# A two-layer FNet and sliding-window attention kernel: the Newton steps of attention's row norms move to GpSimd, the far scores' region is preset once, rows are asked for four visits ahead, and even visits do their norm step at their end

## The chip, the cores and the metric

The kernel runs on one core of a Trainium2 chip. The core has a matrix engine (TensorE, PE in the profile; the loading of its weights is listed as PEld), a vector engine (VectorE, DVE), a scalar engine (ScalarE, ACT), GpSimd (POOL), and SyncE (SP), which issues nearly all DMA transfers here. The metric is the device time of one execution in microseconds (us); lower is better. Matrices collect their sums in PSUM, which the matrix engine writes and which DVE and ACT read; everything else on the chip lies in SBUF.

## The reference

Four blocks over a stream `x` of 2048 rows by 640 columns, each with a layer norm in front and a residual sum behind: spectral mixing, attention, spectral mixing, attention.

```python
def _A_ref(x, dft_seq_re, dft_seq_im, dft_hid_re, dft_hid_im):      # spectral
    a = jnp.einsum("bsd,ed->bse", x, dft_hid_re)
    b = jnp.einsum("bsd,ed->bse", x, dft_hid_im)
    return jnp.einsum("ts,bse->bte", dft_seq_re, a) - jnp.einsum("ts,bse->bte", dft_seq_im, b)

def _B_ref(x, wqkv, wo):                                            # attention, 32 heads of 20, window 256
    ...
    scores = jnp.einsum("bhqd,bhkd->bhqk", q, k) * (Dh ** -0.5)
    mask = (idx[:, None] - idx[None, :] >= 0) & (idx[:, None] - idx[None, :] < W)
    scores = jnp.where(mask[None, None], scores, -1e9)
    p = _softmax(scores, axis=-1)
    o = jnp.einsum("bhqk,bhkd->bhqd", p, v)
    return (...) @ wo

x = A_x
x = x + _A_ref(_layernorm(x), ...)
x = x + _B_ref(_layernorm(x), B_wqkv, B_wo)
x = x + _A_ref(_layernorm(x), ...)
x = x + _B_ref(_layernorm(x), B_wqkv, B_wo)
```

Two things of it matter below. A layer norm needs 1/sqrt(variance + eps) of every row. And a query at row t sees the 256 keys that end at t: for a tile of 128 queries these lie in three tiles of 128 keys, its own, the one before it, and a triangle of the one before that (the *far* tile). The first two query tiles have no far tile.

## The kernel before, in words

**Stages.** Spectral mixing (`spectral`) takes 0 to 555 us of the span and again some 1060 to 1565 us; attention (`attention`) takes the rest. The change is in attention alone, which runs twice; both runs are called the first and the second attention.

**Visits.** Attention is one loop, `for G in range(...)`, and each pass is called a visit here, numbered from 0 to 127 (`g` = 2G counts pairs of heads). A visit treats one query tile and four heads. Sixteen visits make a block `b` of 256 rows, with two query tiles that alternate: even visits take the first, odd visits the second. In visit G the matrix engine computes

- the scores of visit G by query (`scores`): into `sq` for the two near key tiles, and for the far tile into the first 256 columns of `sk`, the region that the code calls `farq`,
- the scores of visit G-8 by key (`by_key`), into the other columns of `sk`, which ACT turns into probabilities (L1212, `ptq`) and GpSimd cuts to the window (`affine_select`, L1216 and L1218),
- on odd visits the product of probabilities and values (`values`, `pf<-ptq,v`) of visits G-11 and G-10, and
- one *fill*: a unit of 15 dense matmuls that has nothing to do with the visit. A fill is a sixth of the query or key projection of a block to come (called QK: `pf<-early,big`, 128x256), a quarter of its value projection (V: `pf<-big,early`, 128x320), or half an output projection of a finished tile (OUT: `pf<-bo,ot`).

DVE takes the largest score of each query (`largest`): for each of two halves, `copy_predicated` (L1156) lays the far scores over the masked triangle of the diagonal tile, and a `tensor_reduce` (L1158) takes the maximum. There is one `sq` buffer per half, so the matrix engine can write the scores of the next visit only when DVE has reduced those of this one. In visits 0 to 15, whose queries have no far tile, the copy reads `neg`, a constant tile in SBUF.

**Row norms.** Blocks 0 and 1 of the rows are made ready before attention begins. For each of the blocks 2 to 7, `rows_norm` makes the normalised rows from which QK and V fills are computed: two tiles of 128 rows are loaded (`x<-x2d`), `norm_steps` takes mean and variance (L139, L142), then 1/sqrt by a guess from the bits (L148, L149) and three Newton steps of two `tensor_scalar` on one column each (L151, L152), then the rows are scaled (L166), split in a high and a low half (`rx`, ACT L177 and GpSimd L178) and turned by a transposing DMA (`early<-rx`).

**What sets the order.** The code is written in order of visits, and a scheduling layer then places each engine's instructions. `norm_steps` is a generator: each `yield` ends a step, and `slow_step` runs one step. `STEPS` says how many steps a visit runs: one in even visits, two in odd ones, and one more in each of visits 0 to 6. `slow_step` holds its instructions behind the visit's last reduction (`topped[0]`) and behind ACT's last listed instruction. A block's norm starts four units of `g` (two visits) after its rows were asked for; in visit 0 the rows of block 2 are asked for at once. Which fill a visit gets is worked out when the program is written: a unit is ready once its rows have a due visit behind them (`done`, set `TURN_LAG` = 6 units after the transposing DMA), and the ready one with the earliest `due` is taken. A visit without a ready unit gets no fill.

The output projection's sum with the residual stream, L935 (`x<-pf,beta,x`), frees the PSUM buffer of an OUT fill; there are two such `pf` buffers, shared by all fills, the values and the small transposes.

Of the kernel before, what the change touches and what calls it, by code (L numbers as in the profile page):

```python
# [46 lines left out]
STEPS = ((1, 2), (1, 2))  # L47
# [3 lines left out]
FREE_STEPS = 4  # L51
PIECES = 2
# [20 lines left out]
def body(ctx: ExitStack, tc: tile.TileContext, x_in, cmat, whid, wqkv, wo, out):  # L73
# [15 lines left out]
    neg = pers.tile([P, P], F32, name="neg")  # L89
# [4 lines left out]
    def constants():  # L94
        make_identity(nc, idf[:])
        nc.vector.tensor_copy(idh, idf)
        nc.gpsimd.memset(mask, 1)
        nc.gpsimd.memset(neg, NEG)
        nc.gpsimd.memset(shift, SHIFT)
        for k in range(2):  # L100
            nc.gpsimd.memset(ones[:, k], M_UP if k else 0.0)
            nc.sync.dma_start(ones_d[k].rearrange("a (b c) -> (a b) c", c=2 * NP * QB // P), ones[:, k])
        nc.gpsimd.affine_select(out=mask, in_=mask, pattern=[[1, P]], base=0, channel_multiplier=-1,
                                compare_op=OP.is_gt, fill=0.0)
# [27 lines left out]
    def norm_steps(xs, ys, act=False):  # L132
# [13 lines left out]
        for k in range(n):  # L146
# [677 lines left out]
    def attention(layer, proj, dst, final):  # L824
        with ExitStack() as st:
# [12 lines left out]
            tps = [t[:, 2 * P:].rearrange("p (a e c) -> p e a c", a=3, e=2) for t in kst]  # L838
            in_turn[0] = True
# [82 lines left out]
            def out_tile(i):  # L922
                ot = OT[i]
                x3 = x2 = X2.pop(i)
                for n in range(2):
# [9 lines left out]
                    nc.vector.scalar_tensor_tensor(x3[:, cs], pf[:, :320], beta, x2[:, cs], op0=OP.mult, op1=OP.add)  # L935
# [66 lines left out]
            def rows_norm(b, x2s):  # L1002

                ys = []
                yield from norm_steps(x2s, ys)
# [143 lines left out]
            def largest(G, pi):  # L1149
# [4 lines left out]
                far = farq[pi] if i >= 2 else neg[:, None, :].to_broadcast([P, 2, P])  # L1154
                with in_line("dve"):
                    marks["dve"] = nc.vector.copy_predicated(near[pi][:, :, 0], mask[:, None, :].to_broadcast([P, 2, P]), far).ins  # L1156
# [140 lines left out]
            def slow_step():  # L1297
                with tc.issue_after(topped[0]), in_line("act"):
# [19 lines left out]
            for G in range(NS // 2 + 1):  # L1318
# [38 lines left out]
                if wanted and x2s and g >= x2s[0] + 4 * (g > 0):  # L1357
                    slow.append(rows_norm(wanted.pop(0), x2s.pop()))
                    x2s.clear()
# [19 lines left out]
                for _ in range(STEPS[layer][G % 2] + (g < ROWS_STEP)):  # L1379
                    slow_step()  # L1380
# [18 lines left out]
                if ran and turned_back:  # L1399
                    with in_line("dve"):  # L1400
                        back(turned_back.pop())
            while unit[0] is not None or fill or slow or idle or later:
# [39 lines left out]
```

## Time and profile before

| | |
|---|---|
| median of 3 runs (lowest, highest) | 2056.11 us (2054.0, 2058.06) |
| the profiled execution's own time | 2055.16 us |
| its span, first to last instruction | 2053.4 us |
| first attention, scores from | 555.5 us on |
| second attention, scores from | 1565.4 us on |
| mean granted TensorE clock | 0.996 |

The time and the span of the profiled execution differ by 1.8 us that lie outside the instructions. In the views below a row of the timeline gives start, duration, engine, line, operation and tiles, with the idle time of the engine ahead of it and what ended that in square brackets. A row of the view of windows gives, for a stretch of time, its length and then each engine's busy time with its number of instructions, the granted clock of the matrix engine, and the share of the DMA engines. A row of the groups gives busy time in us and the mean of one instruction in ns behind the first bar.

### The profile page before, as it was taken

What the parts mean: (1) busy time and instruction counts of PE and PEld (TensorE: products, weight loads), DVE (VectorE), ACT (ScalarE), POOL (GpSimd) and SP (SyncE); (2) the same over time, 40 slices, a digit from 0 to 9 for tenths busy, and PEclk for the clock granted to TensorE, in tenths of its full rate; (3) what the DMA queues carried; (4) which work ended last, traced back from release to release, by engine and by line L of the source; (5) the groups of instructions that cost most, each with busy time, mean ns of one, the idle gap of its engine ahead of it and who ended that gap; (6) DMA issues with size and microseconds to landing.
All of it is one profiled execution on the core that took longest, in us unless ns stands there. A gap on an engine that the chain in (4) does not pass through costs nothing.

```text
span 2053.4 us, 55784 instructions
## 1 busy us (share of the span) xinstructions
PE 1987.5 (97%) x21881; PEld 1449.1 (71%) x21881; DVE 1563.3 (76%) x3261; ACT 1115.0 (54%) x1973; POOL 1469.2 (72%) x2162
## 2 busy tenths in 40 slices
PE   6999999999999999999999999999999999999998
PEld 4777777776767777777667777777677677777765
DVE  8888778768688888777638779787777788887682
ACT  5544555533347677666654444444332567766674
POOL 5777788877557788776557778777783677777653
PEclk9999999999999999999999999999999999999999
DMA  7556566566544444434535565454844455443222
GB/s 274 178 197 202 175 209 228 179 240 216 154 108 111 121 122 121 103 85 111 158 132 179 171 165 186 147 174 139 300 148 131 99 118 123 124 120 98 76 68 72
DMA packets 280508, 311.10 MB, mean 152 GB/s; under 512 B 107572, under 2 KB 214836, under 8 KB 271156
## 3 DMA queue, kind: packets, MB, share of 16 engines
q1 hardware_dynamic: 279668, 306.88, 50.2%
q8 instruction: 171, 2.80, 0.6%
q14 instruction: 93, 0.76, 0.1%
q10 hardware_dynamic: 576, 0.66, 0.1%
HBM read 201.72 MB, written 83.46 MB: 139 GB/s over the span
## 4 chain that ended last, share of the span: by engine, by line
PE 68%; DVE 16%; issue 5%; POOL 4%; ACT 4%; DMA 3%; SPq 0%; DVEq 0%; ACTq 0%; POOLq 0%
PE pf L126 32%; PE y L126 10%; PE x L126 10%; PE z L126 7%; PE sk L126 5%; DVE cc L536 4%; PE sq L126 3%; DVE sq L1156 2%; DVE m L1158 2%; DMA res<-accd 2%; ACT ptq L1212 2%; DVE lnst L139 1%; DVE res L559 1%; DVE lnt L151 1%; POOL cs L526 1%
## 5 line engine op out<-in xcount | busy, mean ns | idle before, releaser
L126 PEld LDWEIGHTS <-cc 128*128 128x128 f16 x5376 | 524.4, 98 | 214.4 <-issue 14.7
L1212 ACT ACTIVATE ptq<-sk,shift,alpha 128x768 f32<-128x768 f32 (+2 forms) x512 | 471.9, 944 | 125.9 <-PE sk L126 74.7
L126 PEld LDWEIGHTS <-big 128*128 128x128 f16 x4320 | 414.3, 98 | 129.3 <-issue 24.2
L1158 DVE TENSOR_REDUCE m<-sq 128x2 f32<-128x512 f32 (+1 forms) x512 | 345.5, 675 | 19.1
L533 ACT ACTIVATE cc<-cs 128x512 f16<-128x512 f32 x256 | 153.6, 624 | 261.4 <-POOL cs L526 150.4
L126 PE MATMUL pf<-early,big 128*128 128x256 f16 x2400 | 292.8, 276 | 0.1
L126 PE MATMUL y<-zc,cc 128*128 128x320 f16 x1728 | 262.8, 299 | 3.2 <-DVE pf L559 3.2
L1216 POOL TENSOR_SCALAR_AFFINE_SELECT ptq<-ptq 128x512 f32<-128x512 f32 x224 | 142.1, 634 | 172.5 <-ACT ptq L1212 171.4
L536 DVE SCALAR_TENSOR_TENSOR cc<-cs,cc 128x512 f16<-128x512 f32 x256 | 248.0, 978 | 6.9 <-ACT cc L533 6.8
L1156 DVE COPY_PREDICATED sq<-mask,sk 128x256 f32<-128x256 int32 x448 | 189.5, 423 | 53.4 <-PE sq L126 51.7
L536 DVE SCALAR_TENSOR_TENSOR cc<-cq,cc 128x512 f16<-128x512 f32 x192 | 205.5, 1072 | 0.1
L126 PE MATMUL pf<-ptq,v 128*32 128x128 f32 (+1 forms) x3840 | 184.4, 330 | 5.1 <-DVE x L935 2.7
L126 PE MATMUL z<-zc,cc 128*128 128x320 f16 x1152 | 177.7, 299 | 6.6 <-DVE res L559 6.6
L1218 POOL TENSOR_SCALAR_AFFINE_SELECT ptq<-ptq 128x512 f32<-128x512 f32 x256 | 164.8, 644 | 18.8 <-ACT ptq L1212 18.6
L126 PE MATMUL x<-zc,cc 128*128 128x320 f16 x1152 | 177.7, 299 | 0.0
L365 ACT ACTIVATE qf<-pf 128x256 f32<-128x256 f32 x160 | 61.1, 382 | 163.7 <-PE pf L126 112.4
L126 PEld LDWEIGHTS pf<-ptq,v 128*32 128x32 f32 x3840 | 110.9, 110 | 48.4 <-DVE x L935 3.9
L126 PE MATMUL pf<-big,early 128*128 128x320 f16 x960 | 141.4, 300 | 0.0
L525 POOL TENSOR_TENSOR cs<-cq 128x512 f32<-128x512 f32 x64 | 86.7, 1355 | 69.5 <-DVE cc L536 68.8
L126 PEld LDWEIGHTS <-qs 62*128 62x128 f16 x2688 | 90.1, 94 | 56.6 <-issue 53.1
L126 PE MATMUL pf<-bo,ot 128*128 128x320 f16 x840 | 123.8, 299 | 2.1 <-DVE big L286 1.2
L126 PE MATMUL x<-big 128*128 128x320 f16 x825 | 122.3, 299 | 2.0 <-DVE big L425 2.0
(142 smaller groups left out, 3481.6 us busy)
## 6 DMA issues: line engine op xcount, KB each, us to landing
cq<-in_cmat_dram SPq DMA_DIRECT2D x64, 1024.0 KB
accd<-res SPq DMA_DIRECT2D x96, 320.0 KB
res<-accd SPq DMA_DIRECT2D x96, 320.0 KB
x<-x2d SPq DMA_DIRECT2D x64, 320.0 KB
qkd<-early SPq DMA_DIRECT2D x160, 128.0 KB
ks<-qkd SPq DMA_DIRECT2D x108, 160.0 KB
qs<-qkd SPq DMA_DIRECT2D x84, 160.0 KB
x2d<-res SPq DMA_DIRECT2D x32, 320.0 KB
```

Of the source, the lines that this page charges most:

```text
L126: i = getattr(nc.tensor, what)(*args, **kw)
L139: nc.vector.bn_stats(st[:, h], x[:, h * 320:(h + 1) * 320])
L151: ts(u, g, g, h, op0=OP.mult, op1=OP.mult)
L365: nc.scalar.activation(f, pf[:, :QB], AF.Copy, scale=down)
L525: g.tensor_tensor(s1, a21, a22, op=OP.add)
L533: nc.scalar.activation(cc[m][:, 0], f, AF.Copy, scale=C_UP)
L536: nc.vector.scalar_tensor_tensor(cc[m][:, 1], f, C_UP, cc[m][:, 0], op0=OP.mult, op1=OP.subtract)
L1156: marks["dve"] = nc.vector.copy_predicated(near[pi][:, :, 0], mask[:, None, :].to_broadcast([P, 2, P]), far).ins
L1158: marks["dve"] = nc.vector.tensor_reduce(TOP[n][:, pi, :, k], near[pi][:, :, :1 + (i >= 1)], axis=AX.XY, op=OP.max).ins
L1212: marks["act"] = nc.scalar.activation(o[:, pi], tps[pi][:, :, first:], AF.Sigmoid, bias=shift, scale=alpha[:, 0:1]).ins
L1216: nc.gpsimd.affine_select(out=q[:, :, a0], in_=q[:, :, a0], pattern=[[0, 4], [-1, P]], base=0, channel_multiplier=1, compare_op=OP.is_gt, ...
L1218: ins = nc.gpsimd.affine_select(out=q[:, :, a0 + 2], in_=q[:, :, a0 + 2], pattern=[[0, 4], [1, P]], base=0, channel_multiplier=-1, compare ...
```

## The change

1. `norm_steps` takes an engine, `roots`. With it the two columns of variances are treated by one pair of guess instructions on DVE (L147 and L148 of the changed file, 128x2), and the three Newton steps are `tensor_scalar` on that engine. `rows_norm` hands it `nc.gpsimd`. The number of steps of one norm stays 13. The other norms are as before.
2. The `neg` tile is gone. The far region of `sk` is set to NEG once, by two `memset` on DVE when attention begins, and `copy_predicated` always reads it.
3. `NORM_LAG` = 8 units of `g` (four visits) stand between the request for a block's rows and its norm. In visit 0 they are asked for as before.
4. Odd visits run two steps in mid-visit (three in visits 1, 3 and 5), even visits one, at the end of the visit. Before, even visits ran one in mid-visit, and two in visits 0, 2, 4 and 6.
5. `slow_step` also holds its instructions behind the last L935 (`marks["x"]`).

```diff
-STEPS = ((1, 2), (1, 2))
+STEPS = 2
...
+NORM_LAG = 8
...
-    neg = pers.tile([P, P], F32, name="neg")
...
-    def norm_steps(xs, ys, act=False):
+    def norm_steps(xs, ys, act=False, roots=None):
...
-        for k in range(n):
+        if roots is not None:
+            h, g = t[:, 0], t[:, 1]
+            ts(h, mv[:, :, 1], 1e-5, -0.5 * X_UP ** -2, op0=OP.add, op1=OP.mult)
+            ts(g.bitcast(I32), h.bitcast(I32), -0.5, ROOT, op0=OP.mult, op1=OP.add)
+            yield
+            for m in range(3):
+                for k in range(n):
+                    h, g, u = (t[:, m, k:k + 1] for m in range(3))
+                    roots.tensor_scalar(u, g, g, h, op0=OP.mult, op1=OP.mult)
+                    normed[0] = roots.tensor_scalar(g, u, 1.5, g, op0=OP.add, op1=OP.mult).ins
+                yield
+        for k in range(0 if roots is not None else n):
...
+            for f in farq:
+                nc.vector.memset(f, NEG)
...
-                    nc.vector.scalar_tensor_tensor(x3[:, cs], pf[:, :320], beta, x2[:, cs], op0=OP.mult, op1=OP.add)
+                    marks["x"] = nc.vector.scalar_tensor_tensor(x3[:, cs], pf[:, :320], beta, x2[:, cs], op0=OP.mult, op1=OP.add).ins
...
-                yield from norm_steps(x2s, ys)
+                yield from norm_steps(x2s, ys, roots=nc.gpsimd)
...
-                far = farq[pi] if i >= 2 else neg[:, None, :].to_broadcast([P, 2, P])
                 with in_line("dve"):
-                    marks["dve"] = nc.vector.copy_predicated(near[pi][:, :, 0], mask[:, None, :].to_broadcast([P, 2, P]), far).ins
+                    marks["dve"] = nc.vector.copy_predicated(near[pi][:, :, 0], mask[:, None, :].to_broadcast([P, 2, P]), farq[pi]).ins
...
-                with tc.issue_after(topped[0]), in_line("act"):
+                with tc.issue_after(topped[0]), in_line("act"), in_line("x"):
...
-                if wanted and x2s and g >= x2s[0] + 4 * (g > 0):
+                if wanted and x2s and g >= x2s[0] + NORM_LAG * (g > 0):
...
-                for _ in range(STEPS[layer][G % 2] + (g < ROWS_STEP)):
-                    slow_step()
+                if G % 2:
+                    for _ in range(STEPS + (g < ROWS_STEP)):
+                        slow_step()
...
+                if G % 2 == 0:
+                    slow_step()
```

Line numbers of the changed file are higher by up to 14: L139 becomes L138, L365 becomes L375, L881 becomes L893, L1156 and L1158 become L1167 and L1169, L1212 becomes L1223.

**Where instructions move: the fills of visits 13 to 15.** A fill's result leaves PSUM by an instruction on ACT: L365 (L375) for QK, L881 (L893) for V. These are ACT's rows of the first attention from the V fill of visit 12 on, in the kernel before:

```order
L881 ACTIVATE v<-pf 128x16x20
L1212 ACTIVATE ptq<-sk_6971,shift,alpha 128x2x256
L1177 ACTIVATE ht<-pf 16x128
L1212 ACTIVATE ptq<-sk_6970,shift,alpha 128x2x256
L1244 ACTIVATE pvs<-pf 128x256
L365 ACTIVATE qf<-pf 128x256
L1212 ACTIVATE ptq<-sk_6971,shift,alpha 128x2x128
L1212 ACTIVATE ptq<-sk_6970,shift,alpha 128x2x128
L365 ACTIVATE qf<-pf 128x256
L1212 ACTIVATE ptq<-sk_6971,shift,alpha 128x2x256
```

and the same place in the changed kernel:

```order
L893 ACTIVATE v<-pf 128x16x20
L1223 ACTIVATE ptq<-sk_6969,shift,alpha 128x2x256
L1188 ACTIVATE ht<-pf 16x128
L1223 ACTIVATE ptq<-sk_6968,shift,alpha 128x2x256
L1004 ACTIVATE bo_66<-wst,wsc 128x640
L1255 ACTIVATE pvs<-pf 128x256
L1223 ACTIVATE ptq<-sk_6969,shift,alpha 128x2x128
L1223 ACTIVATE ptq<-sk_6968,shift,alpha 128x2x128
L1223 ACTIVATE ptq<-sk_6969,shift,alpha 128x2x256
L1188 ACTIVATE ht<-pf 16x128
L1223 ACTIVATE ptq<-sk_6968,shift,alpha 128x2x256
L1255 ACTIVATE pvs<-pf 128x256
```

Visits 13, 14 and 15 each had a QK fill and have none now: the rows of block 2 are due three visits later. QK fills take the places of V fills in visits 16, 18 and 20, those V fills move to visits 27 to 29, and visit 30, which had a QK fill, has none. The matrix engine's order has the missing units back as a second or third fill in visits 65, 75 and 91, in both attentions; from visit 92 on as many units have run as before.

**DVE in the first norm.** In the first attention DVE's rows between the reductions of visit 4 and those of visit 5 were, in the kernel before (the first norm's Newton steps):

```order
L151 TENSOR_SCALAR lnt<-lnt 128x1
L148 TENSOR_SCALAR lnt<-lnmv 128x1
L152 TENSOR_SCALAR lnt<-lnt 128x1
L149 TENSOR_SCALAR lnt<-lnt 128x1
L151 TENSOR_SCALAR lnt<-lnt 128x1 x2
L152 TENSOR_SCALAR lnt<-lnt 128x1 x2
L1156 COPY_PREDICATED sq_6968<-mask,neg 128x256
```

In the changed kernel the first norm's statistics stand after visit 5 and its guesses after visit 6:

```order
L138 BN_STATS lnst<-x_7003 128x6
L138 BN_STATS lnst<-x_7004 128x6
L141 BN_AGGR lnmv<-lnst 128x2
L138 BN_STATS lnst<-x_7004 128x6
L1167 COPY_PREDICATED sq_6966<-mask,sk_6968 128x256
L141 BN_AGGR lnmv<-lnst 128x2
L1169 TENSOR_REDUCE m<-sq_6966 128x2
L1167 COPY_PREDICATED sq_6967<-mask,sk_6969 128x256
L1169 TENSOR_REDUCE m<-sq_6967 128x2
L147 TENSOR_SCALAR lnt<-lnmv 128x2
L148 TENSOR_SCALAR lnt<-lnt 128x2
```

So the norm begins two visits later and puts two small instructions for both row tiles on DVE where there were sixteen; the scaling (L166, L176 now) stood in visit 5 and stands in visit 9.

**GpSimd in the second norm.** In the changed kernel the Newton steps of a norm stand on GpSimd as one block of twelve, here the second norm of the first attention, between the largest scores' `tops` and the copies of a QK fill (`early`) and of attention's output (`os`):

```order
L1179 TENSOR_TENSOR tops_76<-mf,tops_76 128x2x4
L153 TENSOR_SCALAR lnt<-lnt 128x1 x2
L154 TENSOR_SCALAR lnt<-lnt 128x1 x2
L153 TENSOR_SCALAR lnt<-lnt 128x1 x2
L154 TENSOR_SCALAR lnt<-lnt 128x1 x2
L153 TENSOR_SCALAR lnt<-lnt 128x1 x2
L376 CAST early<-qf 128x256
L154 TENSOR_SCALAR lnt<-lnt 128x1 x2
L377 TENSOR_TENSOR early<-qf,early 128x256
L1274 CAST os<-o 128x2x80
```

Before, nothing stood between the `tops` and the copies.

More of the change, by code (lines that the diff above doesn't have):

```diff
@@ L97, in constants @@
         nc.gpsimd.memset(mask, 1)
-        nc.gpsimd.memset(neg, NEG)
         nc.gpsimd.memset(shift, SHIFT)
```

## The prediction

> **What bounds the kernel now.** I read the page first, then stretches of attention, then who waits for whom, then single visits.
>
> ```profile
> span 2053.4 us, 55784 instructions
> PE 1987.5 (97%) x21881; PEld 1449.1 (71%) x21881; DVE 1563.3 (76%) x3261; ACT 1115.0 (54%) x1973; POOL 1469.2 (72%) x2162
> ```
>
> The matrix engine is busy 97% of the span. Busy is not the same as full, so I went to stretches of attention, of the columns PE, PEld, DVE, ACT, POOL, clock:
>
> ```profile
> core 0: us, PE busy (x) PEld busy (x) DVE busy (x) ACT busy (x) POOL busy (x), PEclk, DMA share, GB/s
> 600.00:650.00 50.00, 47.05 (x654) 34.15 (x646) 43.80 (x105) 33.23 (x64) 34.76 (x74) 0.97 0.38 92
> 700.00:750.00 50.00, 49.35 (x783) 36.85 (x779) 44.63 (x116) 36.10 (x57) 38.69 (x85) 1.00 0.44 116
> 1700.00:1750.00 50.00, 50.00 (x794) 37.20 (x793) 41.28 (x97) 34.97 (x55) 36.83 (x84) 1.00 0.48 109
> 904.18:911.30 7.12, 7.12 (x122) 5.31 (x116) 4.84 (x11) 4.97 (x8) 4.81 (x12) 1.00 0.07 20
> 907.11:911.30 4.19, 4.19 (x82) 3.24 (x77) 2.40 (x6) 2.74 (x6) 2.26 (x6) 1.00 0.01 2
> ```
>
> Past its start, attention is bound by the matrix engine. The last two rows are an undisturbed pair of visits and its odd half: 7.12 us with a V and a QK fill, the engine never idle. There, work taken off DVE buys nothing; DVE is worth something only where the matrix engine waits for it:
>
> ```profile
> PE sq L126 <- DVE m L1158: 5.7, 9, 1.5
> PE pf L126 <- DVE x L935: 2.5, 6, 0.8
> PE sq L126 <- DVE m L1158: 4.3, 5, 1.5
> PE pf L126 <- DVE x L935: 1.5, 4, 0.8
> ```
>
> (the first attention, then the second: total us, times, longest.) Some 14 us of waits in all are what the change can win by itself. The longest, in visits 6 and 7:
>
> ```profile
> 575.45 1.81 PE L126 MATMUL pf<-early,big 128*128 128x256 f16 x15
> 578.78 0.21 PE L126 MATMUL sq<-ks 62*128 62x128 f16 x1 [1.52 <-DVE m L1158]
> 580.00 0.38 PE L126 MATMUL sq<-ks 62*128 62x128 f16 x7 [1.00 <-DVE m L1158]
> ...
> 576.24 1.67 POOL L178 TENSOR_TENSOR rx<-lny,rx 128x640 f16<-128x640 f32 x1
> ...
> 576.58 1.62 DVE L1156 COPY_PREDICATED sq<-mask,neg 128x256 f32<-128x256 int32 x1
> 578.30 0.42 DVE L1158 TENSOR_REDUCE m<-sq 128x2 f32<-128x256 f32 x1
> ```
>
> DVE comes late from the first norm, and its copy from `neg` then takes 1.62 us beside GpSimd's `rx`. And a wait of this kind costs more than itself:
>
> ```profile
> 575.23:585.63 10.40, 7.87 (x63) 5.81 (x64) 6.62 (x13) 2.67 (x6) 8.12 (x14) 0.84 0.54 121
> 1584.26:1593.01 8.75, 6.22 (x64) 4.95 (x65) 6.63 (x13) 2.67 (x6) 7.46 (x13) 1.00 0.42 111
> 581.24:584.66 3.42, 3.42 (x19) 2.44 (x17) 1.33 (x3) 0.60 (x2) 2.74 (x5) 0.50 0.74 158
> 608.55:611.96 3.41, 3.41 (x24) 2.35 (x17) 2.86 (x8) 0.79 (x2) 1.35 (x5) 0.50 0.27 82
> 1615.48:1618.89 3.41, 3.41 (x27) 2.19 (x17) 2.94 (x9) 0.95 (x2) 1.44 (x5) 0.50 0.27 79
> ```
>
> The first two rows are visits 6 and 7 of either attention: both idle 2.53 us, but the first is 1.65 us longer, since the clock stood at 0.50 for 3.42 us right behind the waits. This happened once more in each attention, in visit 15. A stretch of 3.41 us with much idle time is followed by one at half clock, worth 1.7 us where the engine has dense work.
>
> **The change part by part.** The prices of the small instructions:
>
> ```profile
> L151 DVE TENSOR_SCALAR lnt<-lnt 128x1 f32<-128x1 f32 x192 | 50.8, 269 | 4.1
> L152 DVE TENSOR_SCALAR lnt<-lnt 128x1 f32<-128x1 f32 x192 | 39.6, 211 | 4.0
> L148 DVE TENSOR_SCALAR lnt<-lnmv 128x1 f32<-128x1 f32 x64 | 9.1, 142 | 0.2
> L1156 DVE COPY_PREDICATED sq<-mask,neg 128x256 f32<-128x256 int32 x64 | 33.5, 523 | 16.2 <-PE sq L126 16.2
> L1156 DVE COPY_PREDICATED sq<-mask,sk 128x256 f32<-128x256 int32 x448 | 189.5, 423 | 53.4 <-PE sq L126 51.7
> L1166 POOL TENSOR_SCALAR mf<-m 128x8 f32<-128x8 f32 x128 | 33.8, 264 | 9.4 <-DVE m L1158 6.3 <-DVE lnt L148 2.2 <-PE pf L126 0.3
> L1167 POOL CAST tops<-mf 128x8 f16<-128x8 f32 x128 | 25.1, 196 | 7.5
> ```
>
> *DVE.* Six norms an attention, two tiles each, so 24 tiles. The Newton steps leave: 24 x 3 x (0.269 + 0.211) = 34.6 us. Of 48 guess instructions 24 stay, 3.4 us less at 0.142. The 64 copies from `neg` fall to the mean of those from `sk`: 64 x 0.100 = 6.4 us. Four `memset` come; the nearest row, the reduction of 256 columns above, has 0.42 us, so 1.7 us, ahead of the first scores, when DVE has nothing to do. DVE loses some 43 us; by the rows above nearly all of it lies beside the matrix engine.
>
> (a) *The first norm's waits.* The norm starts two visits later, runs fewer steps a visit and has no Newton steps on DVE, and the copies no longer read `neg`. From the order: behind visit 5's reductions DVE still has four statistics instructions, some 1.6 us, so visit 7's scores wait about 1.1 us in the first attention (where `bo` is also split on DVE) and 0.5 in the second. Against 2.5 each before, and 0.9 more in the first attention (its nine waits are 5.7 us; less these 2.5 and some 1.8 in visits 13 to 15, 1.4 are left, of which I count 0.9 here): -2.3 and -2.0. The half clock of visit 7 was worth 1.65 in the first; I count 0.7 of it: -1.2.
>
> (b) *Visits 13 to 15 without fill.*
>
> ```profile
> 599.96:612.50 12.54, 10.75 (x131) 7.67 (x126) 10.71 (x34) 6.05 (x14) 6.26 (x15) 0.86 0.44 96
> 1606.97:1619.51 12.54, 10.96 (x130) 7.66 (x126) 10.71 (x34) 6.13 (x14) 6.27 (x15) 0.86 0.43 99
> 608.75 3.37 PE L126 MATMUL pf<-early,big 128*128 128x256 f16 x15
> 571.85 3.45 PE L126 MATMUL pf<-early,big 128*128 128x256 f16 x30
> 966.32:969.03 2.71, 2.48 (x63) 1.85 (x59) 2.57 (x6) 2.38 (x4) 1.44 (x4) 1.00 0.32 122
> ```
>
> They took 12.54 us, with the second norm on DVE, 1.6 to 1.8 us of idle matrix engine and the half clock (3.37 us for a fill that takes 1.81). A fill is worth 3.45 - 1.81 = 1.64 us. The nearest visit without one is the last row, odd: 2.71 us. The even visit 14 reduces half as much, 2 x (0.69 - 0.42) us less (0.69 is a reduction of 512 columns at 580.84, quoted below): 2.2. So the three now take 2.71 + 2.2 + 2.71 = 7.6 us, and their fills come back in visits that are full: 3 x 1.64 = 4.9. Sum 12.5: nothing lost. But the matrix engine now has 4.3 us of work in these 7.6 (12.54 less 4.92 of fills, 1.6 to 1.8 idle and 1.56 of half clock), idle nearly as much of it as ahead of the half clocks. I take one stretch of half clock in each, partly hidden by DVE: +1.1, between 0 and 3.4.
>
> ```profile
> 580.84 0.69 DVE L1158 TENSOR_REDUCE m<-sq 128x2 f32<-128x512 f32 x1
> 659.60:662.25 2.65, 2.57 (x45) 2.13 (x41) 2.44 (x8) 2.33 (x3) 2.39 (x6) 1.00 0.57 151
> 734.24:739.11 4.87, 4.39 (x80) 3.29 (x76) 4.26 (x11) 3.40 (x6) 3.48 (x6) 1.00 0.24 82
> 835.14:840.52 5.38, 4.57 (x81) 3.32 (x76) 3.77 (x9) 3.41 (x6) 3.15 (x6) 1.00 0.77 152
> 612.50:639.01 26.51, 25.39 (x356) 18.34 (x351) 22.89 (x50) 18.52 (x37) 19.73 (x41) 1.00 0.22 65
> ```
>
> (c) *Visit 30 without fill* (second row): it took 2.65 us with a QK fill and, by the 2.71 above, takes that without. Its 1.64 us come back later as pure loss. Half clock behind 1.6 us of idle: even odds of 1.7. Together +2.5 in each attention.
>
> (d) *The slow step behind L935.* Visits 51 and 79 (the next rows) are 0.7 and 1.2 us over the 4.19 of an odd visit, 59 and 75 by 0.4 each: a norm's scaling had gone ahead of the sum that frees `pf`. That is 2.6 us in the first attention and 1.9 in the second, which lacks visit 51. I take three quarters: -2.0 and -1.4.
>
> (e) Visit 91 now has three fills, two of them OUT, and must wait for L935 within itself: +0.5 each, by the 0.8 us of the longest such wait. (f) Visits 16 to 23 (last row) idle 1.1 us; without Newton steps on DVE about half: -0.6, and -0.1 in the second.
>
> (g) *GpSimd* gets 72 instructions an attention. None of this form is in the trace; the nearest, 8 columns wide, take 0.196 and 0.264. A block of twelve is 2.4 to 3.2 us, between the `tops` and the copies of QK and `os`, with the cuts of the probabilities queued behind. GpSimd is free 7.12 - 4.81 = 2.31 us in each pair, so it falls behind for one or two pairs. What it makes is used two visits later (cuts) or more, so the cover is about 7 us less what it takes anyway; I take 0.4 an attention, between 0 and one us for each of the six blocks. DVE's scaling, which now waits for GpSimd, stands at least a visit behind the block.
>
> Sum, first attention: -2.3 - 1.2 + 1.1 + 2.5 - 2.0 + 0.5 - 0.6 + 0.4 = -1.6. Second: -2.0 + 1.1 + 2.5 - 1.4 + 0.5 - 0.1 + 0.4 = +1.0. Together -0.6 on the profiled execution's 2055.16; as that lies 0.95 under the median, **2055.5 us** for the median of the changed kernel: no change that can be told, which begins at about 0.2%, 4.1 us.
>
> **The rivals.**
>
> *The clock holds (faster).* If no new stretch of half clock comes, (b) gives 0 and (c) 1.64: 2 x (1.1 + 0.85) = 3.9 less. With (d) whole, 1.1 less, and the half clock of visit 7 surely gone, 0.5 less, and (g) nothing, 0.8 less, it is 2055.5 - 6.3 = 2049.2. For it: the visits from 113 on lack every second fill, and the row at 966.32 shows clock 1.00. Against it: they have a full fill between. The Trainium skill (TensorE: Matmul & The Clock Gate, "Why this matters for your kernels") has the clock fall only when the engine idles for a gap over about 3 us; by that rule this rival is the likeliest. The trace disagrees: the gaps at 578.78 and 580.00 are 1.52 and 1.00 us, and half clock followed. I give it 0.28.
>
> *The clock falls at every empty place (slower).* Half clock in full behind visits 13 to 15, and a second time there, and behind visit 30: 2 x (3.4 - 1.1) + 2 x 0.85 = 6.3 more, 2061.8. It decides where the engine idles more than some half of a 3.41 us stretch; before, each attention lost it once in visit 15 at 1.6 to 1.8 us of idle. Chance 0.16.
>
> *GpSimd becomes the bound (slower).* If one Newton instruction takes twice L1166, a block is 12 x 0.53 = 6.3 us, nearly the 7 us in which the cuts are wanted; with 2.31 us free in a pair the matrix engine would wait 1 to 1.5 us in each of twelve blocks: 12 to 18 us, 2070. The wait would show as `pf<-ptq,v` behind POOL. Against it are the 0.196 and 0.264. The Trainium skill (GPSIMD Engine Reference, "Engine selection") tells to keep elementwise work on VectorE, GpSimd being about half as fast with two tensor inputs and about as fast with one; a Newton instruction has one and two scalars, so an estimate from that page and DVE's mean of 0.24 us is 2.9 us a block by the one half of the rule and 5.8 by the other. No run so far shows it for one column. Chance 0.10.
>
> *The relief goes nowhere.* DVE's late instructions hang on something else than the norm, the waits of visit 6 and 51 stay, and (a), (d) and (f) give nothing: 2055.5 + 3.5 + 2.0 + 3.4 + 0.7 = 2065.1. The waits' rows name DVE, and DVE's rows there are the norm's, so 0.02.
>
> **How the numbers follow.** Forecast 0.44, its own range 2052 to 2060. Faster is the first rival, 0.28; slower the other three, 0.28; the same 0.44. The range takes in the two clock rivals and stops short of 2070: 2048.5 to 2063, leaving out some 0.1 above and a little below.
>
> **What would show it.** Of the changed kernel: visits 6 and 7 of either attention under 8 us in place of 10.40 and 8.75, and their waits at most half; visits 13 to 15 near 7.6 us in all with no `pf<-early,big`; visit 30 still 2.65; visits 65, 75 and 91 longer by 1.6, 2.0 and 4 us or more; no wait of `pf<-ptq,v` for L935 in visits 51 and 79; granted clock 0.50 in a stretch at visits 14 to 16, perhaps at 31. It is wrong if the matrix engine idles in places that aren't named here, if twelve Newton steps take over 4 us on GpSimd, or if the clock's stretches come at other places than behind idle ones.

## The result, and the profile after

The changed kernel takes 2068.22 us in the median of five runs (2063.2 to 2069.86), the kernel before 2056.11 in the five runs beside them: a ratio of 1.0057, 95% interval 1.0043 to 1.0071. It is some 12 us slower. Forecast was 2055.5 with a range of 2048.5 to 2063. The profiled execution is the fastest of the five, 2063.2 us; the head of its page, and the groups of the Newton steps:

```profile
span 2061.4 us, 55786 instructions
PE 1990.4 (97%) x21881; PEld 1451.2 (70%) x21881; DVE 1531.8 (74%) x3097; ACT 1112.8 (54%) x1973; POOL 1501.0 (73%) x2305
```

```profile
L153 POOL TENSOR_SCALAR lnt<-lnt 128x1 f32<-128x1 f32 x72 | 23.9, 340 | 1.2 <-DVE lnt L148 1.2
L154 POOL TENSOR_SCALAR lnt<-lnt 128x1 f32<-128x1 f32 x72 | 18.2, 264 | 0.0
```

DVE lost 31.5 us of busy time and GpSimd gained 31.8; a block of twelve Newton instructions takes, by these means, 6 x (0.340 + 0.264) = 3.6 us there. The matrix engine, whose work is the same, is busy 2.9 us longer, and the rest of the 8.0 us of span is idle time. Now the stretches that matter here (visits 6 and 7 of either attention, 13 to 15 of either, then of the first attention 16, 79, 30, 31, 91 and 62):

```profile
574.36:580.45 6.09, 6.09 (x65) 4.86 (x65) 4.35 (x12) 1.42 (x4) 5.37 (x18) 1.00 0.43 108
1589.73:1595.82 6.09, 6.09 (x63) 4.84 (x64) 4.19 (x11) 1.42 (x4) 5.25 (x17) 1.00 0.40 105
594.75:602.41 7.66, 5.45 (x82) 3.24 (x78) 6.68 (x15) 5.71 (x12) 4.66 (x10) 0.81 0.85 119
1610.13:1617.20 7.07, 4.72 (x82) 2.89 (x78) 5.85 (x14) 5.16 (x11) 3.98 (x10) 1.00 0.84 114
602.41:607.05 4.64, 3.17 (x43) 2.31 (x40) 3.76 (x8) 2.12 (x5) 2.02 (x6) 0.94 0.86 228
837.88:842.07 4.19, 4.19 (x80) 3.25 (x76) 2.64 (x7) 2.66 (x5) 4.03 (x11) 1.00 0.47 114
650.92:653.54 2.62, 0.83 (x30) 0.70 (x26) 2.35 (x5) 1.87 (x2) 1.22 (x3) 1.00 0.53 126
653.54:659.49 5.95, 5.95 (x81) 4.08 (x77) 2.48 (x7) 2.78 (x5) 2.75 (x8) 0.71 1.00 231
880.37:889.13 8.76, 8.43 (x110) 6.13 (x106) 3.83 (x9) 2.66 (x5) 4.46 (x11) 1.00 0.67 181
767.41:776.43 9.02, 5.33 (x46) 3.14 (x42) 3.15 (x7) 2.04 (x3) 3.10 (x7) 0.65 0.90 234
```

Most of this is as predicted: visits 6 and 7 run without idle time (10.40 and 8.75 before), the three empty visits take 7.66 and 7.07, visit 30 keeps its length, visit 79 is down from 5.38 to 4.19. What was not predicted is the last row. Visit 62 took 2.92 us before, and takes 9.02:

```profile
774.93:777.85 2.92, 2.92 (x45) 2.06 (x41) 2.71 (x8) 2.33 (x3) 2.57 (x7) 1.00 0.87 201
```

Some waits of the matrix engine after the change, of the first attention and then of the second, and behind them a row of either before it:

```profile
PE sk L125 <- ACT ptq L1223: 4.7, 7, 1.8
PE pf L125 <- DMA ot<-os: 3.7, 1, 3.7
...
PE pf L125 <- DMA early<-rx: 1.3, 1, 1.3
PE pf L125 <- POOL tops L1179: 1.1, 2, 0.9
...
PE sq L125 <- DVE m L1169: 0.7, 2, 0.4
```

```profile
PE sk L125 <- ACT ptq L1223: 8.3, 14, 2.0
...
PE pf L125 <- POOL tops L1179: 1.1, 2, 0.9
PE sq L125 <- DVE m L1169: 1.0, 3, 0.4
```

```profile
PE sk L126 <- ACT ptq L1212: 0.8, 3, 0.4
...
PE sk L126 <- ACT ptq L1212: 4.3, 9, 2.0
```

The waits for DVE's largest scores (`m`), 5.7 and 4.3 before, have nearly gone (0.7 and 1.0). Two kinds of wait have come in their place. Of the 4 us more behind ACT's `ptq` in either attention 3.5 lie in the visits without a fill, 13 to 15 and 30: there the matrix engine has too little of its own to do, as the prediction had counted. The other kind it had not: in the first attention two waits for transposes by the DMA, which the kernel before did not have. The one in visit 62, first in SP's queue (what the second load waited for, then the queue) and then on the matrix engine:

```profile
SPq L198 <- DMA qkd<-early: 3.5, 1, 3.5
...
762.11 0.38 SPq L198 DMA_DIRECT2D qkd<-early  x1
766.12 0.72 SPq L198 DMA_DIRECT2D qs<-qkd  x2
766.89 2.03 SPq L206 DMA_TRANSPOSE ot<-os  x1
...
771.48 4.18 PE L125 MATMUL pf<-bo,ot 128*128 128x320 f16 x15 [3.69 <-DMA ot<-os]
```

The change puts the last QK fill of the next block into visit 58 and an OUT fill into visit 62 (an OUT and a V fill before). The QK fill's store is issued at 762.11. The load that reads it back, behind it in the queue, waits 3.5 us for that store and is issued 4.0 us after it, and the transpose that the OUT fill needs stands behind that load. The fill starts 4.6 us after the transpose's issue, and takes 4.18 us in place of the 2.21 of the same fill elsewhere: it runs at half clock.

### The profile page after: what moved, and what is told of

The parts are those of the page before. It is cut to its first block, busy times and chain, and to the rows that moved or that the text cites. A ratio compares the mean times of both kernels' runs of the same rounds, so it can differ in the third digit from the quotient of the medians.

```text
span 2061.4 us, 55786 instructions
## 1 busy us (share of the span) xinstructions
PE 1990.4 (97%) x21881; PEld 1451.2 (70%) x21881; DVE 1531.8 (74%) x3097; ACT 1112.8 (54%) x1973; POOL 1501.0 (73%) x2305
## 4 chain that ended last, share of the span: by engine, by line
PE 69%; DVE 12%; POOL 6%; issue 5%; ACT 4%; DMA 4%; SPq 0%; DVEq 0%; ACTq 0%; POOLq 0%
PE pf L125 33%; PE y L125 10%; PE x L125 10%; PE z L125 7%; PE sk L125 5%; DVE cc L546 4%; PE sq L125 3%; ACT ptq L1223 2%; DMA res<-accd 2%; DVE sq L1167 1%; DVE res L569 1%; DVE m L1169 1%; POOL cs L536 1%; POOL ptq L1229 1%; DVE lnst L138 1%
## 5 line engine op out<-in xcount | busy, mean ns | idle before, releaser
L1223 ACT ACTIVATE ptq<-sk,shift,alpha 128x768 f32<-128x768 f32 (+2 forms) x512 | 471.6, 944 | 154.5 <-PE sk L125 85.6
L1169 DVE TENSOR_REDUCE m<-sq 128x2 f32<-128x512 f32 (+1 forms) x512 | 345.6, 675 | 19.4 <-POOL tops L1178 0.5
L125 PE MATMUL pf<-early,big 128*128 128x256 f16 x2400 | 288.6, 274 | 1.9 <-DMA early<-rx 1.6
L1167 DVE COPY_PREDICATED sq<-mask,sk 128x256 f32<-128x256 int32 x512 | 216.9, 424 | 84.0 <-PE sq L125 82.1
L375 ACT ACTIVATE qf<-pf 128x256 f32<-128x256 f32 x160 | 61.1, 382 | 154.1 <-PE pf L125 104.5
L125 PEld LDWEIGHTS <-ot 128*128 128x128 f16 x960 | 90.6, 99 | 54.2 <-issue 8.6
```

Source lines behind the costliest of these rows:

```text
L125: i = getattr(nc.tensor, what)(*args, **kw)
L375: nc.scalar.activation(f, pf[:, :QB], AF.Copy, scale=down)
L1169: marks["dve"] = nc.vector.tensor_reduce(TOP[n][:, pi, :, k], near[pi][:, :, :1 + (i >= 1)], axis=AX.XY, op=OP.max).ins
L1223: marks["act"] = nc.scalar.activation(o[:, pi], tps[pi][:, :, first:], AF.Sigmoid, bias=shift, scale=alpha[:, 0:1]).ins
```

## The experiments

**Theory T**: the loss is in the moved fills: empty visits, the half clock behind them, and transposes that come late for the fills which now need them. **R1**: GpSimd's Newton blocks hold up its later work and, through SP's queue, the transposes. **R2**: the norm step at an even visit's end costs. The first four kernels take the change apart.

*The whole change but for the lag* (`NORM_LAG = 8` -> `4`):

> The whole change with NORM_LAG back at 4: Newton steps on GpSimd, preset, step rule and the new mark stay. By the order, only visit 13 is without its fill in either attention (the whole change: 13, 14, 15 and 30), visit 29 and 30 keep theirs, and visit 91 has two fills in place of three. Theory T (the loss is in the moved fills: the empty visits, the half clock behind them, the transposes that come late in visits 16 and 62): the gains of visits 3 to 9 (5.3 and 2.7 us) and of 51 and 79 (0.7 and 1.2, 1.2) stay, visit 30 with its half clock (3.1 us in each attention) and the 6.1 us of visit 62 are not there: about 2049, between 2046 and 2054. Rival R1 (GpSimd's Newton blocks of 3.6 us push its later work, and through SP's queue the transposes): all twelve blocks are here too, so it stays where the whole change is, 2062 to 2068. Rival R2 (the step at the end of an even visit costs): also 2062 or more.

Measured: 2052.9 us, ratio 0.9988 (0.9979 to 0.9998). As T had it, and a miss for R1 and R2, which leave their cause in the kernel. It doesn't refute them by itself: two larger effects, a relief of DVE worth some 12 us and a step rule that costs some 9, turn out below to stand against each other in this kernel.

*The lag alone*, in the kernel before:

```diff
-                if wanted and x2s and g >= x2s[0] + 4 * (g > 0):
+                if wanted and x2s and g >= x2s[0] + 8 * (g > 0):
```

> The kernel before with the one number 4 in the norm's condition made 8; the Newton steps stay on DVE. By the order, visits 13, 14 and 29 have no fill in either attention, and visit 91 has three. T: slower than before, by the two half clocks behind the empty visits (1.7 each) and some of the late transposes, without any gain on DVE: 2059 to 2066. R1: no Newton step on GpSimd, so as before, 2056, within 3. R2: the step rule is untouched, as before.

Measured: 2066.41 us, 1.0062 (1.0048 to 1.0076), just past the slow end of T; R1 and R2, which had it as before, miss. Its trace shows the empty visits: 13 to 15, 29 and 30 of either attention hold three fills less than before and are together only 1.3 and 1.2 us shorter, while visits 75 and 91, which have the fills back, are 6.9 us longer in either. In visit 30 the matrix engine waits 1.9 and 1.7 us for a transpose of the norm's rows (`early<-rx`).

*The step rule alone*, in the kernel before (odd visits two steps, and a third where `g < ROWS_STEP`; even visits one at the end):

> The kernel before with the step rule alone: odd visits two steps (three up to step 14 of a block), even visits one, at their end. By the order, only visit 13 is without its fill, and visit 91 has two. T: within 4 us of before, 2053 to 2060, visit 62 in the first attention under 4 us. R1: as before. R2 (the even visit's step at its end is what costs): 2062 or more.

Measured: 2063.66 us, 1.0043 (1.0031 to 1.0056). That is a miss for T, which had 2053 to 2060, and looks like R2. The trace shows the place. Visits 13 to 15 of either attention, and then, in the order of time, the transposes of the first norm's rows on SP's queue and the QK fill of visit 14:

```profile
597.29:612.23 14.94, 9.28 (x115) 6.34 (x110) 9.26 (x24) 6.27 (x14) 5.53 (x13) 0.77 0.58 137
1609.65:1623.07 13.42, 8.92 (x114) 6.13 (x110) 8.79 (x22) 5.63 (x13) 5.10 (x12) 0.87 0.63 131
```

```profile
592.25 2.21 SPq L196 DMA_TRANSPOSE early<-rx  x1
598.11 1.59 SPq L196 DMA_TRANSPOSE early<-rx  x1
605.14 3.36 PE L126 MATMUL pf<-early,big 128*128 128x256 f16 x15 [4.51 <-DMA early<-rx]
```

and the same two transposes in the kernel before:

```profile
582.59 2.21 SPq L196 DMA_TRANSPOSE early<-rx  x1
590.83 2.06 SPq L196 DMA_TRANSPOSE early<-rx  x1
```

Only visit 13 lost its fill, but the three visits, one fill lighter, take longer than the 12.54 us before. The rows are turned 7 to 10 us later, the fill of visit 14 waits 4.51 us for them (7.0 us from issue to start), and then runs at half clock. The planner that gives the fills counts visits between a transpose and its use, and visit 13 without its fill lasts only 1.96 us by the starts of its scores. Why are the rows late? `g < ROWS_STEP` holds in visits 0 to 6 of an attention alone. There the old rule ran five norm steps in a pair of visits and the new one runs four. That the fewer steps cost, and not the place of the even one, is still only argued here.

*The other three edits alone*: Newton on GpSimd, the preset, the mark of L935, in the kernel before:

> The kernel before with the Newton steps on GpSimd, the preset region and the slow step behind L935, but lag 4 and the step rule of before. By the order, every fill stands in the visit that it had before. T: the DVE waits of visits 3 to 9 shrink and nothing is lost: faster than before by 3 to 8 us, 2048 to 2053. R1: the twelve blocks on GpSimd cost what the whole change lost and the relief of DVE besides: slower than before, 2060 to 2070. R2: as T, since the step rule is that of before.

Measured: 2042.78 us, 0.9941 (0.9929 to 0.9954), 12 us **faster**, better than T's range. All twelve blocks on GpSimd are in this kernel, so R1 is refuted. Visits 6 and 7 of its first attention:

```profile
576.48:582.55 6.07, 6.07 (x63) 4.89 (x64) 3.76 (x8) 2.18 (x6) 5.83 (x11) 1.00 0.17 51
```

The three ratios add up: -0.59% and +0.43% and +0.62% make +0.46%, against +0.57% (0.43 to 0.71) for the whole change. The relief of DVE is worth more than I had forecast, and the lag and the step rule give back more than all of it.

*The changed kernel once more*, unedited:

> The changed kernel once more, unedited, for a second profiled execution; its first one had a span of 2061.4 while the repeats went up to 2068.1. If the 6.1 us of visit 62 in the first attention (a transpose of `os` that stood behind a blocked load in SP's queue) belong to the order, they are there again, and the second attention, which has the same fills in visits 58 and 62, may show them too: span 2061 to 2068. If they were an accident of that execution, visit 62 takes under 4 us and the span is near 2056 unless something else is late.

Measured: 2062.39 us, span 2060.7. Visit 62 of the first attention has it again, 8.33 us; the second attention again has not. So the stall belongs to the order. The queue is held in the second attention too: in the first profiled execution the load that reads the result back is issued 3.45 us after the store (1775.34 and 1778.79). But no transpose of `os` stands close behind it there (the nearest are issued at 1738.69 and 1787.54), and visit 62 takes 2.92 us. Visit 62 of the first attention and its OUT fill in the second execution:

```profile
770.34:778.67 8.33, 4.39 (x46) 2.61 (x41) 2.78 (x6) 2.04 (x3) 3.10 (x7) 0.80 0.97 232
```

```profile
774.66 3.62 PE L125 MATMUL pf<-bo,ot 128*128 128x320 f16 x15 [3.94 <-DMA ot<-os]
```

Three kernels then test what the loss of the step rule and of the lag hangs on. The first repairs only the pace of the step rule (its text says "of a block"; the step is counted from the attention's start, so visits 1, 3 and 5 are meant):

```diff
-                    for _ in range(2 + (g < ROWS_STEP)):
+                    for _ in range(2 + 2 * (g < ROWS_STEP)):
```

> The kernel before with the step rule (the even visit's step at its end), but four steps in place of three in odd visits up to step 14 of a block: five a pair of visits as before, not four. By the order, every fill stands where it was before. Theory T, sharpened by the three runs on single edits: the step rule lost its 8.9 us not by where the even step stands but by one step fewer a pair, which brings the transposes of the first norm's rows some 8 us later, so that the fill of visit 14 waits for them (5.0 and 3.9 us idle there) and the clock halves: now not slower than before, 2049 to 2056. Rival R2 (the place of the even step at the visit's end costs): still near 2063.

Measured: 2051.05 us, 0.9979 (0.9967 to 0.9991). The 8.9 us are gone and 3.5 more with them; the even step still stands at the visit's end, so R2 is refuted too. The second takes the changed kernel and repairs only the lag of the norms that start in visits 0 to 15, which are the first two of either attention (the second takes its statistics in visit 14 in place of 19):

```diff
-                if wanted and x2s and g >= x2s[0] + NORM_LAG * (g > 0):
+                if wanted and x2s and g >= x2s[0] + (NORM_LAG if g >= 2 * NP else 4) * (g > 0):
```

> The changed kernel with the old lag of 4 for the norms that start within the first block of either attention, 8 for all later ones. By the order, its fills stand almost as in the kernel with the lag of 4 throughout: visit 13 empty, 14, 15 and 30 filled, visit 91 with two. T (the lag costs only because the first norms start later and everything behind them is late): about the 2052.9 of the lag of 4 throughout, 2049 to 2056. Rival R3 (rows asked for four visits ahead cost in the steady run, by their loads or buffers): stays above 2060.

Measured: 2055.19 us, 1.0000 (0.9988 to 1.0013). Of the 12 us nothing is left, although every later norm keeps the lag of 8: R3 is refuted. Which of the first two norms the lag costs by was not tried apart. What this kernel still loses is the pace, visible in its visits 13 to 15 of the second attention:

```profile
1605.57:1622.05 16.48, 10.03 (x116) 6.69 (x112) 8.45 (x22) 6.01 (x13) 5.03 (x13) 0.69 0.65 110
```

The third has both repairs:

> The changed kernel with both repairs: lag of 4 for the norms that start in the first block and four steps in place of three in odd visits up to step 14. Newton on GpSimd, the preset, the mark, the even step at the visit's end and the lag of 8 for all later norms stay. By the order, every fill stands where it was before. T: as the kernel with the relief of DVE alone, 2042.8, or a little less by visits 51 and 79: 2038 to 2046. R2 or R3: above 2050.

Measured: 2038.58 us, 0.9920 (0.9903 to 0.9936): 16 us faster than the kernel before and 30 faster than the change. All five edits are in it, two of them altered at the start of each attention. Head of its page, visits 13 to 15 of either attention, and visit 79:

```profile
span 2035.6 us, 55785 instructions
PE 1976.3 (97%) x21881; PEld 1445.0 (71%) x21881; DVE 1533.8 (75%) x3097; ACT 1113.3 (55%) x1973; POOL 1501.9 (74%) x2305
```

```profile
596.49:607.42 10.93, 9.10 (x130) 6.84 (x125) 9.60 (x24) 6.67 (x15) 6.26 (x14) 1.00 0.69 173
1596.62:1606.82 10.20, 9.30 (x129) 6.89 (x125) 8.59 (x23) 6.19 (x14) 5.80 (x14) 1.00 0.61 147
828.07:832.58 4.51, 4.37 (x81) 3.31 (x77) 3.51 (x8) 2.67 (x5) 4.34 (x10) 1.00 0.96 154
```

All three fills are in these visits, as before, in 10.93 and 10.20 us in place of 12.54.

*What the stall of visit 62 hangs on*: the changed kernel with `HOLD = 2` -> `4`.

> The changed kernel with HOLD = 4 in place of 2: the loads of stacks, and whatever else is held, are put into SP's queue one visit later; every fill stays where the change has it. In both profiled executions of the change, visit 62 of the first attention lost 3.7 and 3.9 us, and half clock behind: the OUT fill there waited for a transpose of `os` that stood in SP's queue behind a load `qs<-qkd`, which itself waited for the store of a QK fill that the change had moved to visit 58. If that reading holds, the transpose now goes first, visit 62 takes under 4 us, and the first attention gains about 6; what the later loads cost elsewhere is open, so the time is 2060 to 2066 if they cost little. If the transpose was late by itself, visit 62 stays at 8 to 9 us.

Measured: 2085.07 us, 1.0142 (1.0119 to 1.0165). The transpose now goes ahead of the load (760.98 against 767.61), visit 62 is back at 2.92 us and its OUT fill at 2.21, so the reading of its stall held. The forecast of the time, 2060 to 2066, missed. Behind visit 63's fill the matrix engine now waits for a load (the OUT fill of visit 62, and the scores that wait):

```profile
768.43 2.21 PE L125 MATMUL pf<-bo,ot 128*128 128x320 f16 x15
```

```profile
778.82 0.27 PE L125 MATMUL sk<-ks,qs 62*128 62x128 f16 x3 [3.83 <-DMA qs<-qkd]
```

This wait makes visit 63 last 8.20 us, so the first attention gained nothing: 462.80 us by the starts of its first and last visit, 461.96 in the change. It is not the load that held the queue: that one was issued at 767.61, just behind the landing of its store, this one at 773.92, with no store left to wait for. What is new for it is that every held load now goes a visit later. So the run shows what stalled visit 62, and does not show whether an earlier QK fill would have cured it. The kernels without a QK fill in visit 58 don't settle that: with the lag of 4, visit 62 takes 2.92 us with an OUT fill in it, but there the transpose too is issued much earlier, at 752.26. The other 17 us that the later loads cost I did not follow further; 12.8 of them are in the second attention, by the same starts.

*Which edit relieves*: Newton on GpSimd alone, and the preset with the mark alone.

> The kernel before with the Newton steps on GpSimd alone: copies from `neg` stay, the slow step doesn't wait for L935's sum, lag and step rule are those of before, and so is every fill's place. The three edits (Newton, preset, mark) brought -12.0 together. T: the Newton steps are most of DVE's relief (34.6 of some 43 us), and so of the gain: 2044 to 2050. Rival R4 (the preset is what counts, since the longest wait stood behind a copy from `neg` of 1.62 us): within 4 of before.

> The kernel before with the preset and the mark alone; the Newton steps stay on DVE, and every fill where it was. T: some 6.4 us of DVE less and one long copy gone: 2050 to 2055. R4: 2042 to 2047. If the edits add up, this and the kernel with the Newton steps alone together are 12 us under twice the time before.

Measured: 2047.24 us, 0.9962 (0.9949 to 0.9975), and 2046.37 us, 0.9960 (0.9949 to 0.9972). Either kernel alone is some 8 us faster, with all three edits 12: they do not add up. T had Newton right and the preset too small, and R4 had the preset right but not that Newton brings as much. The waits of the first attention, Newton alone and then the preset with the mark:

```profile
PE sq L126 <- DVE m L1169: 5.7, 8, 1.8
PE pf L126 <- DVE x L946: 2.2, 6, 0.5
```

```profile
PE pf L124 <- DVE x L935: 2.5, 6, 0.8
PE sq L124 <- DVE m L1157: 2.3, 6, 0.8
```

With the copies from `neg` the longest wait for DVE stays near what it was (1.8 us, 1.5 before); without them it is 0.8 us. And the mark does nothing for the wait behind L935: 2.5 us in six waits, as before. The preset and the mark were not run apart, but what this kernel gains stands where the mark can hold nothing: visits 6 and 7 (6.42 us in either attention; 10.40 and 8.75 before) and 13 to 15 (10.81 in both; 12.54 before) come before the first OUT fill, in visit 32, and so before the first L935.

*Newton back on VectorE*, in the kernel with both repairs (`roots=nc.vector`):

> The kernel with both repairs (2038.6), with the Newton steps, in the same groups, on VectorE in place of GpSimd. T (the gain is DVE's relief, GpSimd has the room): slower than 2038.6 by 3 to 10 us. Rival R1, what is left of it (GpSimd's blocks of 3.6 us cost something by themselves, and the grouping is the gain): as fast or faster, 2035 to 2039.

Measured: 2043.64 us, 0.9948 (0.9936 to 0.9960), against 0.9920 on GpSimd, each beside its own runs of the kernel before. GpSimd is the better place by 5 us, though each instruction takes longer there (340 and 264 ns, 269 and 211 on DVE). The prediction weighed a rule of the Trainium skill (GPSIMD Engine Reference, "Engine selection") that speaks for VectorE; these two runs decide against it for this place, where DVE is waited for and GpSimd is not.

## Why the prediction was wrong

**The step that failed is (b)**, in its sentence that the fills of visits 13 to 15 "come back in visits that are full: 3 x 1.64 = 4.9. Sum 12.5: nothing lost". I priced a moved fill by the visit that lost it and by its own 1.64 us. I did not ask, of the fills that now stand elsewhere, what they wait for and who waits for them, although the order showed the QK fills in visits 16, 18 and 20. What was lost there in the first attention is visit 62 (+6.1 us: 3.7 of waiting for the transpose, and the fill at half clock), visit 16 (+1.7, 2.93 to 4.64, waiting for `early<-rx`) and visit 43 (+1.3, of which 0.4 is the longer fill; see (g)); the second attention lost 0.7 in visit 16 and 1.3 in visit 43. The rest of the bookkeeping stands: fills of each kind are as many as before. The deeper cause is the start of each attention, which has no slack. The first norm can't have its rows asked for four visits ahead, since they are asked for in visit 0, so with a lag of 8 it starts two visits later, and the step rule takes a step from each of its pairs. I wrote "The norm starts two visits later", counted that as relief for DVE in (a), and never carried the two visits on to the transposes. The repairs show that the loss hangs on this start: the step rule's on the first norm alone, the lag's on the first two norms, between which no run decides. One of the prediction's own signs of being wrong came true: the matrix engine idles in places that it did not name, visits 62 and 43.

Point by point, by the terms of the sum:

- (a) Right, and too small. Visits 6 and 7: -4.31 and -2.66 us; predicted -3.5 and -2.0. The cause is less single than I wrote, and the gains of the parts overlap. The two visits together, first attention and second, were 10.40 and 8.75 before; they take 6.86 and 6.97 with the lag alone, 6.75 and 6.75 with the step rule alone, 9.97 and 6.27 with the Newton steps alone, 6.42 and 6.42 with the preset and the mark.
- (b) The length of the three visits was right (7.6 predicted; 7.66 and 7.07). The bill behind them was not, as above. With it stands the place of the half clock: predicted at visits 14 to 16 of both, it came from 599.53 us on in the first alone.
- (c) Nearly right: visits 30 and 31 together went from 2.65 + 4.50 to 2.62 + 5.95, +1.42, and the fill came back: 3.1 us, predicted 2.5. The half clock, which I gave even odds, came in both attentions of this execution and in neither of the second one (below).
- (d) Right in size (visit 51 shorter by 0.68 us, visit 79 by 1.19 in both; predicted -2.0 and -1.4 in all, measured -1.9 and -1.2 from these two; visit 59, which the term counts too, is 0.1 and 0.2 longer with another fill, and visit 75 has a fill more), wrong in cause. The preset with the mark leaves visits 51 and 79 as they were (4.89 and 5.39 us). In visit 79 the lag alone does it (4.22), and the Newton steps alone do part of it (4.90); in visit 51 the lag alone (4.33) or the step rule alone (4.19). Visit 79 with the lag alone, and with the Newton steps alone:

```profile
835.13:839.35 4.22, 4.22 (x80) 3.25 (x76) 4.04 (x12) 2.74 (x5) 2.31 (x5) 1.00 0.33 113
```

```profile
834.76:839.66 4.90, 4.40 (x80) 3.29 (x76) 3.29 (x8) 3.42 (x6) 4.10 (x7) 1.00 0.54 132
```

- (e) Right: visit 91 went from 4.37 to 8.76, 4.08 for two OUT fills and 0.3 of waiting; 0.5 predicted.
- (f) Near enough: visits 17 to 23 went from 23.58 to 21.98 and from 22.38 to 21.98 us; 0.7 of either is a QK in place of a V fill in visits 18 and 20, so -0.9 and +0.3, predicted -0.6 and -0.1.
- (g) A block takes 3.6 us where I had 2.4 to 3.2. GpSimd's `tops` come late once, in visit 43 of either attention, where the matrix engine waits 0.85 us for them; what stands ahead of them there is the norm's split (L188, `rx`, 1.40 us from 696.67 on), which the change moved, and no Newton block: the nearest ended at 676.91. Nor does a Newton block run between 752 and 767 us, ahead of visit 62's stall. So no wait behind a Newton block is seen, where I had 0 to 1 us a block, and the last experiment shows that GpSimd is the better place.

The rivals: "GpSimd the bound" (2070) and "the relief goes nowhere" (2065.1) had the nearest times, and both are refuted, the one by the kernel that is 12 us faster with all the blocks on GpSimd, the other by visits 6, 7, 51 and 79. "The clock falls at every empty place" (2061.8) names a part of what happened. No rival had a transfer that becomes the wait, which is what the traces show.

The first and second attention of the profiled execution lose 6.4 and 3.5 us by the starts of visit 127, and what lies outside visits 0 to 126 gives 2.0 back. The other four runs of the change are 1 to 7 us longer than that execution. Where they lose it is open; the second profiled execution was no longer than the first.

## What to carry to other kernels

Before a step is delayed, find the instances of it that have no slack, here those at the start of a loop, and follow its result to the first instruction that reads it; a rule that fits the steady run can cost more at the start than it wins in all the rest. Where units of work are moved by a planner, price what each moved unit waits for and who waits for its result, not only its own time and the gap it leaves. When edits are measured together and the sum is near zero, take them apart: here the same change held 12 us of gain and some 20 of loss, and two small edits kept the one without the other.

## What the runs showed of the hardware

**The clock is decided on a fixed grid.** All stretches at 0.50 start on a grid of 3.413 us: in the change at 599.53, 654.14, 770.20 and 1667.90 us, which are 16, 34 and 263 steps apart, and the longer ones are two or three steps. What counts is the idle time of the matrix engine within one step. Visit 30 shows it, since it idles 1.79 us in one piece in both profiled executions of the change. In the first its piece lay within one step, 3.41 less 1.62 us idle, and the next stood at half clock:

```profile
650.73:654.14 3.41, 1.62 (x51) 1.31 (x49) 2.53 (x7) 2.31 (x4) 1.82 (x4) 1.00 0.64 141
654.14:657.55 3.41, 3.41 (x38) 2.01 (x33) 2.14 (x4) 2.02 (x4) 1.82 (x5) 0.50 1.21 243
```

In the second the border fell into it, 0.37 us idle on one side and 1.43 on the other, and the clock held:

```profile
651.27:654.68 3.41, 3.04 (x41) 2.26 (x40) 1.53 (x5) 1.49 (x4) 2.14 (x7) 1.00 0.84 121
654.68:658.09 3.41, 1.98 (x49) 1.50 (x52) 2.81 (x6) 2.70 (x5) 1.71 (x3) 1.00 0.85 156
```

Over the attention of the fourteen profiled executions here (to 2010 us), taken step by step at full clock: of 23 steps with 1.75 us or more idle, 22 were followed by half clock; of 21 with 1.35 to 1.75, six; of some 3800 with less, none. So in these runs a step that was idle for about half cost the next step half its speed, and whether one gap did that depended on where the grid fell. In the two executions of the change it lay 0.54 us apart (650.73 and 651.27), and visit 31 took 5.95 us in the one and 4.32 in the other: that is one source of the spread between runs. The Trainium skill (TensorE: Matmul & The Clock Gate, "What's actually happening") has a window of 3413 ns that runs freely, and the traces agree with it by their grid of 3.413 us. Its rule to avoid gaps over some 3 us ("Why this matters for your kernels") names a longer gap than these runs needed: one of 1.79 us was enough.

**Sixty-four copies.** That the preset would be worth some 8 us I had not expected, as it touches 64 copies of 3261 DVE instructions. The copies' own time, 33.5 + 189.5 us in the rows that the prediction quotes (523 ns each from `neg`, 423 from `sk`), fell by 6.3 in the kernel with the preset and the mark:

```profile
L1155 DVE COPY_PREDICATED sq<-mask,sk 128x256 f32<-128x256 int32 x512 | 216.7, 423 | 68.2 <-PE sq L124 65.5 <-PE pf L124 0.9
```

Their place, in the first visits of each attention, where DVE was what the matrix engine waited for, made them worth more than their time; half clocks that no longer follow are in it too, since this kernel's profiled execution has none in attention before its last microseconds, against three before 2010 us in the kernel before.
